# Linear attention and a gated layer on one core: a new order for the head, chunk 0 alone beside the weight conversion, chunk 1 by seven products

## The chip, the cores and the metric

The kernel runs on one core of a Trainium2 chip. The metric is the device time of one execution in microseconds (us), given as the median of several executions. Profiles come from one execution taken by the hardware profiler. TensorE is called PE in the profile, its weight loads PEld, VectorE DVE, ScalarE ACT, GpSimd POOL, and SyncE, which issues the DMAs, SP.

## The reference

```python
# q, k, v: (8 batches, 8 heads, 576 rows, 64), g_norm: (64,)
kv  = einsum('bhsd,bhse->bhde', k, v)
o   = einsum('bhsd,bhde->bhse', q, kv)
o   = o / sqrt(mean(o * o, axis=-1) + 1e-6) * g_norm
x   = o.transpose(0, 2, 1, 3).reshape(4608, 512)
out = (sigmoid(x @ w_gate) * (x @ w_val)) @ w_out      # w_gate, w_val: (512, 1536), w_out: (1536, 512)
```

q, k and v are float32. The three weight matrices arrive as float64 and are converted to float32 in the kernel by operations on their bits; every matmul is float32.

## The kernel before

**Attention.** Work comes in pairs of heads: n = 4 x batch + pair, n from 0 to 31. `attention(n, at_ps)` returns eleven steps: `kv_mm` (L227, k transposed times v on PE) and `kv_out` (L233, two copies on DVE, which also issues the k and v loads of a later n), `q_mm` (L241, six transposes on PE) and `q_out` (L246, copy on ACT, issues q of a later n), `u_mm` (L256, q times kv on PE), `u_square` (L260, ACT), `u_sum` (L264, DVE), `u_root` (L268, square root on ACT), `u_norm` (L271 and L273, DVE), `x_mm` (L282, transposes on PE) and `x_out` (L291, ACT, writes the columns of `xT`). The matrix x is kept transposed in `xT[c]`, where chunk c is 512 of the 4608 rows. A batch has 576 rows, so chunk 0 lies wholly in batch 0 (n = 0 to 3), and chunk 1 has the last 64 rows of batch 0 and 448 rows of batch 1 (n = 4 to 7). `xT[c][:, m, :]` comes from pair m.

**Weights.** There are 18 units, in `units`: twelve named ("gv", f), each with 128 columns of w_gate and of w_val, and six named ("wo", f) with two blocks of 128 rows of w_out. `load_unit(u)` issues two DMAs (L106) of 512 KB into one of NST = 3 buffers `st`. `convert(u)` gives five steps: s0 (L139 on DVE, then L141 on ACT), s1 (L147 on DVE, L149 on ACT), s2 (L154, DVE), s3 (L158, DVE) and s4 (L163, DVE). Before, s4 of each unit but the first also issues the next load that has not been issued, and s0 and s1 of the unit u + 1 stand in the order ahead of s2 to s4 of unit u.

**Matmuls.** A block (c, f) of the first layer makes 128 columns of the hidden layer for a chunk. In the plain form (`Plain`, L400) it is eight matmuls with 512 columns moving, four (m = 0 to 3) for the gate and four for the value, followed by a sigmoid on ACT (`gate`, L405) and a product on DVE (`end`, L408), which are put into `late` and run amid the next block. The plain second layer (`second_layer`, L385) makes each 128-row tile t of the output by twelve matmuls. The fast form (`first_layer_fast` L526, `second_layer_fast` L606) splits rows, columns and depth in halves and makes seven products in place of eight, each on 256 columns; it needs sums of the weights (`w_sum`, L512, on POOL, for the first layer; `t2w` on DVE, for the second, once for all chunks), sums of x (`x_sums`, L502 to L505, DVE), and sums of the hidden layer (`h_sums`, DVE). Its PSUM tiles are read by DVE at L538 to L559 between two products that add into the same tile, and a block of it ends at L562.

**Order.** The schedule is by hand: each engine works through its own instructions in the order in which the program writes them. Before, `stage(i)` runs the attention steps of the first eight pairs (NE = 8) as a software pipeline, with five conversion steps in the first three stages; then comes block (0, 0), then twenty plain blocks that alternate between chunks 0 and 1, while `convert_some` spreads the conversion over them. Then follow the whole second layer of chunk 0, the last three first-layer blocks of chunk 1 in the plain form, and chunk 1's second layer in the fast form. Chunks 2 to 8 are in the fast form throughout. The attention of the next batch is queued in `fill` by `feed`, and `slot()` takes one entry of it after certain matmuls; for batch 2 the slots lie in chunk 0's second layer and chunk 1's last blocks. The memory of the raw weights (`raw`) is given back after the last conversion step and used by the sums (`sums`).

Of the kernel before, what the change touches and what calls it, by code (L numbers as in the profile page):

```python
# [19 lines left out]
def kernel(  # L20
# [11 lines left out]
    nc = tc.nc  # L32
# [74 lines left out]
            else:  # L107
                nc.sync.dma_start(out=st[:, i], in_=moe_w_out[P * (f + i):P * (f + i) + P, :])

    def load_next_unit():  # L110
        load_unit(len(staged))

    def words(u):
        t = staged[u].rearrange("p i f -> p (i f)").bitcast(U32).rearrange("p (n two) -> p n two", two=2)
        return t[:, :, 0], t[:, :, 1]
# [8 lines left out]
    def convert(u):  # L124
        kind, f = units[u]
        vec = nc.vector
        d = {}

        def s0():

            t = const.tile([P, 2, DM], FP32, name=f"{kind}{f}") if kind == "gv" else w2[:, f:f + 2, :]
            if kind == "gv":
                for i, name in enumerate(("wg", "wv")):
                    w[name, f] = t[:, i].rearrange("p (m f) -> p m f", m=NMT)
            else:
                for i in range(2):
                    w["wo", f + i] = t[:, i]
            d["m"] = m = t.rearrange("p i f -> p (i f)")
            vec.tensor_scalar(out=m.bitcast(U32), in0=words(u)[1], scalar1=0x000FFFFF, scalar2=None,  # L139
                              op0=ALU.bitwise_and)  # L140
            nc.scalar.activation(out=m, in_=m.bitcast(U32), func=AF.Identity, scale=2.0 ** -20, bias=one)  # L141

        def s1():


            d["p"] = p = raw.tile([P, UW], U32, tag="cz", name="cz", bufs=2)
            vec.tensor_scalar(out=p, in0=words(u)[1], scalar1=20, scalar2=0x7FF, op0=ALU.logical_shift_right,  # L147
                              op1=ALU.bitwise_and)
            nc.scalar.activation(out=p.bitcast(I32), in_=p, func=AF.Relu, scale=2.0 ** 23, bias=exp_off)  # L149

        def s2():

            m = d["m"]
            vec.scalar_tensor_tensor(out=m, in0=words(u)[0], scalar=2.0 ** -52, in1=m, op0=ALU.mult, op1=ALU.add)  # L154

        def s3():
            p = d["p"]
            vec.scalar_tensor_tensor(out=p, in0=words(u)[1], scalar=0x80000000, in1=p, op0=ALU.bitwise_and,  # L158
                                     op1=ALU.bitwise_or)

        def s4():
            m = d["m"]
            vec.tensor_tensor(out=m, in0=m, in1=d["p"].bitcast(FP32), op=ALU.mult)  # L163
            if u:
                load_next_unit()

        return [s0, s1], [s2, s3, s4]


    halves_of = [convert(u) for u in range(len(units))]  # L170
    converts, last = deque(), {}
    converts.extend(halves_of[0][0] + halves_of[0][1] + halves_of[1][0])
    last[0] = 5
    for u in range(1, len(units)):
        if u + 1 < len(units):
            converts.extend(halves_of[u + 1][0])
        converts.extend(halves_of[u][1])
        last[u] = len(converts)
    made = [0]

    def convert_some(n):
        for _ in range(min(n, len(converts))):
            converts.popleft()()
            made[0] += 1

    def converted(u):
        convert_some(last[u] - made[0])

    for n in range(4):
        load_kv(n)  # L190
        load_q(n)
        if n == 0:
            load_next_unit()


    w2 = const.tile([P, NFT, DM], FP32, name="w2")
# [6 lines left out]
        nc.scalar.dma_start(out=g_col[HD * e:HD * e + HD], in_=g_norm.rearrange("(d o) -> d o", o=1))  # L203
    make_identity(nc, ident)
    nc.vector.memset(eps, 1e-6)
    for kv in kvs:
        nc.vector.memset(kv, 0.0)

# [90 lines left out]
    def slot():  # L299
        if fill:  # L300
            fill.popleft()()
# [26 lines left out]
    def flush():  # L328
        while fill:
            fill.popleft()()  # L330
# [7 lines left out]
    def sg_tile():  # L338
        return sb.tile([P, G], FP32, tag="sg", name="sg", bufs=4)
# [17 lines left out]
    def at_ps(kind):  # L357
        return psum_at.tile([P, 2, 512], FP32, tag="at", name="at")

    def two(i):  # L360
        return at_ps(None) if i == 3 else psum0.tile([P, 2, 512], FP32, tag=f"two{i}", name="two")

    shared = [None]
    turns = {"u": 1, "qx": 0}

    def early(kind):

        if kind == "q":
            return shared[0]
        tag = "u" if kind == "u" else "qx"  # L370
        t = two(turns[tag] if tag == "u" else 2 + turns[tag])
        turns[tag] = 1 - turns[tag]
        if kind == "kv":
            shared[0] = t
            return t[:, :, JH * P:]
        return t

    def mm_ps():
        return psum.tile([P, 512], FP32, tag="mm", name="mm", bufs=6)

    def second_layer(c):
        for t in range(G // P):
            ps = mm_ps()
            for f in range(NFT):
                nc.tensor.matmul(ps, gv[c, f][:, P * t:P * t + P], w["wo", f], start=(f == 0), stop=(f == NFT - 1))  # L385
                if f % 2:
                    slot()
            ot = sg_tile()
            nc.scalar.copy(out=ot, in_=ps)
            store(c, t, ot)  # L390


    class Plain:
# [15 lines left out]

    late = deque()  # L410

    def finish():
        while late:
            late.popleft()()

    def halves(t):
        return t[:, 0], t[:, 1]

    def plain(c, f, n_convert, ps):

        converted(f)
        blk = Plain(c, f, ps)
        for at in range(2 * NMT):
            i, m = divmod(at, NMT)
            blk.mm(i, m)
            slot()
            if late:
                late.popleft()()
            convert_some(n_convert * (at + 1) // 8 - n_convert * at // 8)
        late.extend([blk.gate, blk.end])  # L430


    KV, KV_OUT, Q, Q_OUT, U, U_SQUARE, U_SUM, U_ROOT, U_NORM, X, X_OUT = range(11)
    a = [attention(n, early) for n in range(NE)]

    def do(n, *steps):
        if 0 <= n < NE:
            for step in steps:
                a[n][step]()

    def stage(i, n_convert):
        do(i, KV, Q, KV_OUT, Q_OUT)
        do(i - 2, U_SUM, U_ROOT, U_NORM)
        do(i - 1, U, U_SQUARE)
        do(i - 3, X, X_OUT)
        convert_some(n_convert)

    for i in range(NE + 1):
        stage(i, 2 if i < 2 else 1 if i == 2 else 0)
        if i + 5 == NE:  # L450
            load_next_unit()
            load_next_unit()
    blk = Plain(0, 0, halves(early("u")))
    for m in range(NMT):
        blk.mm(0, m)
    do(NE - 1, U_SUM, U_ROOT)
    do(NE - 2, X, X_OUT)
    do(NE - 1, U_NORM)
    convert_some(2)
    for m in range(2):  # L460
        blk.mm(1, m)
    do(NE - 1, X, X_OUT)
    for m in range(2, NMT):
        blk.mm(1, m)
    convert_some(2)
    blk.gate()
    first_ctx.__exit__(None, None, None)
    hp = ctx.enter_context(tc.tile_pool(name="hp", bufs=21))
    blk.end()
    blocks = [(1, 0)] + [(c, f) for f in range(1, NFT - 3) for c in range(2)] + [(0, f) for f in range(NFT - 3, NFT)]  # L470
    for n, (c, f) in enumerate(blocks):
        plain(c, f, 5, halves(two(n % 4)))
    assert n % 4 == 3
    finish()
    convert_some(len(converts))
    psum_ctx.__exit__(None, None, None)
    psum = ctx.enter_context(tc.tile_pool(name="psum", bufs=1, space=bass.MemoryType.PSUM))
    raw_ctx.__exit__(None, None, None)


# [149 lines left out]
    def sums_of(c):  # L630
        if c < NG:
            fill.append(lambda: fill.extendleft(reversed(x_sums(c))))


    sums = ctx.enter_context(tc.tile_pool(name="sums", bufs=2, side="right"))
    b12, b11, b21, b22 = (w2[:, NF2 * (j - 1):NF2 * j, DH * (n - 1):DH * n] for j, n in ((1, 2), (1, 1), (2, 1), (2, 2)))
    t2w = {i: sums.tile([P, NF2, DH], FP32, name=f"t2w{i}", bufs=1) for i in (2, 3, 4)}
    t2w[1] = b12
    tt(out=t2w[3], in0=b22, in1=b12, op=ALU.subtract)
    feed(2, at_ps)  # L640
    second_layer(0)
    for n in (1, 2, 3, 4):
        for f in (0, NF2):
            w_sum(f, n)
    for f in range(NFT - 3, NFT):
        plain(1, f, 0, (mm_ps(), mm_ps()))
        if f == NFT - 3:
            tt(out=t2w[1], in0=b12, in1=b11, op=ALU.subtract)
            tt(out=t2w[2], in0=b22, in1=t2w[1], op=ALU.subtract)
            tt(out=t2w[4], in0=b21, in1=t2w[2], op=ALU.subtract)  # L650
            for i in range(NF2 - 3):
                h_sums(1, i)
    finish()
    for i in range(NF2 - 3, NF2):
        h_sums(1, i)
    flush()
    sums_of(2)
    second_layer_fast(1)
    flush()


    for c in range(2, NG):
        if c + 1 < B:
            feed(c + 1, at_ps)
        first_layer_fast(c)
        sums_of(c + 1)
        second_layer_fast(c)
        flush()
# [30 lines left out]
```

## Time and profile before

| What | Value |
|---|---|
| Median of 9 runs | 1128.75 us (1128.31 to 1130.16) |
| Profiled execution | 1128.31 us |
| its span, first to last instruction | 1126.2 us |
| granted PE clock | 1.00 |
| PE busy | 1105.9 us, 98% |
| DVE / ACT / POOL busy | 536.8 / 310.6 / 239.6 us |
| HBM read / written | 47.19 / 9.44 MB |

The span is what the engines' instructions cover; the execution's own time is 2.1 us longer. The page cuts the span into 40 slices of about 28 us and gives the busy share of each engine in tenths. A group line names the source line, the engine, the operation, the tiles written and read, the count, then total busy time, the mean of one in ns and the idle time before it. A line of the chain of waits has the start, the length and what the chain passed through. A line of the timeline has the start, the length, the engine and the instruction, and in brackets how long the engine stood idle before it and what released it. Lines of SPq are DMA issues.

### The profile page before, as it was taken

The numbers are of one execution on the slowest core, as the hardware profiler recorded it, in microseconds if no ns is written. First come the engines' busy times: TensorE is split into PE (matmuls) and PEld (weight loads), VectorE is DVE, ScalarE is ACT, GpSimd is POOL, SyncE is SP. The second block draws the span as 40 slices with busy tenths as digits, with TensorE's granted clock in tenths as the row PEclk, the third lists the DMA queues.
The fourth block names the chain that finished last, engine by engine and source line by source line (L and its number), as shares of the span: only waits on it lengthen the run. The fifth ranks groups of instructions, "written<-read, shape, count | busy, mean of one in ns | idle before, by whom it ended". The sixth has DMA issues, their size and how long they took to land.

```text
span 1126.2 us, 14586 instructions
## 1 busy us (share of the span) xinstructions
PE 1105.9 (98%) x5616; PEld 884.7 (79%) x5616; DVE 536.8 (48%) x1087; ACT 310.6 (28%) x589; POOL 239.6 (21%) x342
## 2 busy tenths in 40 slices
PE   6999999999999999999999999999999999999998
PEld 5644444547888888888888888888888888888887
DVE  4567664054155524562355425551655246615641
ACT  4633340223033303331243113330334021101110
POOL 0000001000033303330133104320333034404420
PEclk9999999999999999999999999999999999999999
DMA  9844331120202012110202120201200000010001
GB/s 244 211 140 134 137 112 36 47 71 14 77 22 54 11 29 63 46 30 19 72 12 54 27 75 12 53 12 42 55 11 6 19 19 1 1 27 12 1 1 38
DMA packets 71588, 57.56 MB, mean 51 GB/s; under 512 B 40800, under 2 KB 65376, under 8 KB 71520
## 3 DMA queue, kind: packets, MB, share of 16 engines
q1 hardware_dynamic: 71360, 56.64, 19.0%
q8 instruction: 45, 0.74, 0.3%
q14 instruction: 23, 0.19, 0.1%
q10 hardware_dynamic: 160, 0.00, 0.0%
HBM read 47.19 MB, written 9.44 MB: 50 GB/s over the span
## 4 chain that ended last, share of the span: by engine, by line
PE 95%; DVE 2%; DMA 1%; ACT 1%; SPq 0%; issue 0%; ACTq 0%; DVEq 0%
PE mm L526 45%; PE mm L606 26%; PE two L400 9%; PE mm L385 4%; PE at L400 3%; PE at L256 2%; PE at L227 2%; PE at L241 1%; PE at L282 1%; PE mm L400 1%; DMA q<-in_q_dram 1%; DMA v<-in_v_dram 1%; PE two L256 0%; DVE sq L273 0%; DVE gv L163 0%; DVE ms L264 0%
## 5 line engine op out<-in xcount | busy, mean ns | idle before, releaser
L512 POOL TENSOR_TENSOR tw<-gv 128x256 f32<-128x256 f32 x168 | 120.6, 729 | 835.7 <-PE mm L526 655.6
L526 PE MATMUL mm<-sx,tw 128*128 128x256 f32 x672 | 159.7, 380 | 0.0
L526 PE MATMUL mm<-xT,tw 128*128 128x256 f32 x672 | 159.5, 380 | 0.0
L526 PE MATMUL mm<-xT,gv 128*128 128x256 f32 x672 | 158.7, 379 | 0.0
L526 PEld LDWEIGHTS mm<-xT,gv 128*128 128x128 f32 x672 | 127.7, 190 | 17.4
L526 PEld LDWEIGHTS mm<-sx,tw 128*128 128x128 f32 x672 | 126.1, 190 | 16.7
L526 PEld LDWEIGHTS mm<-xT,tw 128*128 128x128 f32 x672 | 125.3, 190 | 16.1
L512 POOL TENSOR_TENSOR tw<-gv,tw 128x256 f32<-128x256 f32 x168 | 123.6, 757 | 0.0
L400 PE MATMUL two<-xT,gv 128*128 128x512 f32 x256 | 111.3, 593 | 2.1 <-DVE gv L163 1.6
L400 PEld LDWEIGHTS two<-xT,gv 128*128 128x128 f32 x256 | 48.3, 190 | 62.4 <-issue 61.9
L606 PE MATMUL mm<-t2w,gv 128*128 128x256 f32 x384 | 89.0, 379 | 0.0
L606 PE MATMUL mm<-w,gv 128*128 128x256 f32 x384 | 88.1, 379 | 0.0
L606 PE MATMUL mm<-w,s 128*128 128x256 f32 x384 | 88.1, 379 | 0.0
L555 ACT ACTIVATE sg<-sg 128x256 f32<-128x256 f32 x84 | 35.0, 417 | 191.7 <-DVE sg L554 191.7
L606 PEld LDWEIGHTS mm<-w,s 128*128 128x128 f32 x384 | 73.0, 190 | 9.9
L606 PEld LDWEIGHTS mm<-t2w,gv 128*128 128x128 f32 x384 | 72.6, 190 | 9.7
L606 PEld LDWEIGHTS mm<-w,gv 128*128 128x128 f32 x384 | 72.5, 190 | 9.6
L526 PE MATMUL mm<-sx,gv 128*128 128x256 f32 x336 | 79.4, 379 | 0.0
L546 DVE TENSOR_TENSOR gv<-mm,sg 128x256 f32<-128x256 f32 x84 | 35.7, 425 | 88.9 <-PE mm L526 88.9
L533 ACT COPY sg<-mm 128x256 f32<-128x256 f32 x84 | 31.3, 372 | 141.0 <-PE mm L526 140.9
L526 PEld LDWEIGHTS mm<-sx,gv 128*128 128x128 f32 x336 | 63.1, 190 | 8.2
L562 DVE TENSOR_TENSOR gv<-gv,sg 128x512 f32<-128x512 f32 x84 | 67.2, 840 | 0.2
(93 smaller groups left out, 1150.8 us busy)
## 6 DMA issues: line engine op xcount, KB each, us to landing
k<-in_k_dram SPq DMA_DIRECT2D x32, 288.0 KB, 4.5
v<-in_v_dram SPq DMA_DIRECT2D x32, 288.0 KB, 5.0
q<-in_q_dram SPq DMA_DIRECT2D x64, 144.0 KB, 3.2
st<-in_moe_w_gate_dram SPq DMA_DIRECT2D x12, 512.0 KB, 3.8
st<-in_moe_w_val_dram SPq DMA_DIRECT2D x12, 512.0 KB, 5.0
st<-in_moe_w_out_dram SPq DMA_DIRECT2D x12, 512.0 KB, 4.0
out_dram<-sg SPq DMA_DIRECT2D x24, 192.0 KB, 2.3
out_dram<-sg SPq DMA_DIRECT2D x24, 128.0 KB, 2.3
```

The lines of the kernel that those rows point to most:

```text
L227: nc.tensor.matmul(ps[HD * e:HD * e + HD, 0, 0:HD], pairs[n]["k"][:, e, js], pairs[n]["v"][:, e, js], start=(j == 0), stop=(j == NJ - 1))
L241: nc.tensor.transpose(ps[:, j // JH, c0:c0 + NP], pairs[n]["q"][:, j].rearrange("p e d -> p (e d)"), ident[0:NP, 0:NP])
L256: nc.tensor.matmul(d["u"][:, i], qT[:, M * i:M * i + MU], kvs[n % 2], start=True, stop=True)
L385: nc.tensor.matmul(ps, gv[c, f][:, P * t:P * t + P], w["wo", f], start=(f == 0), stop=(f == NFT - 1))
L400: nc.tensor.matmul(self.ps[i], w[("wg", "wv")[i], self.f][:, m, :], xT[self.c][:, m, :], start=(m == 0), stop=(m == NMT - 1), skip_group_c ...
L512: nc.gpsimd.tensor_tensor(out=tw[f, i], in0=b[in0], in1=b[in1] if isinstance(in1, tuple) else tw[f, in1], op=ALU.subtract)
L526: nc.tensor.matmul(ps, wt[:, m, :], xs[:, m, :], start=(new and m == 0), stop=(m == NK - 1), skip_group_check=True)
L533: nc.scalar.copy(out=d["sg"][:, h2], in_=pa)
L546: tt(out=d["h"][:, h2], in0=pb, in1=d["sg"][:, h2], op=ALU.add)
L555: nc.scalar.activation(out=d["sg"][:, h2], in_=d["sg"][:, h2], func=AF.Sigmoid)
L562: tt(out=d["h"], in0=d["h"], in1=d["sg"], op=ALU.mult)
L606: nc.tensor.matmul(ps, hs(f), ws[:, f, :], start=(new and f == 0), stop=(f == NF2 - 1), skip_group_check=True)
```

## The change

The order of the first eight pairs is now written out as a string of tokens. The number in a token is n: `K0` is `kv_mm` and `q_mm` of pair 0, `KVO0` and `QO0` are its two copies, then `U0`, `SQ0`, `SUM0`, `ROOT0`, `NORM0`, `X0` and `XO0` are the other steps by their names. `c` is the next conversion step, `w1` and `w2` issue the loads of units 1 and 2, and `bfim` (as `b012`) is one matmul of block (0, f): i = 0 for the gate and 1 for the value, m the quarter of the depth. `G` and `E` are the sigmoid and the product of block (0, 0). The PSUM tiles of the head are shared differently: one tile for k, v and q of all pairs, one each for even and odd pairs, and one for block 0.

Conversion now goes unit by unit, five steps each, and s4 of each unit u issues the load of unit u + 3, that of unit 0 included. Blocks 2 to 11 of chunk 0 follow, with one unit converted per block. Chunk 0's second layer then has f outermost: its four output tiles are summed side by side in four PSUM tiles, and the six "wo" units are converted beside it; its last two f are done tile by tile, with the sums of x for chunk 1 in the slots. All of chunk 1 is in the fast form. The `t2w` sums are cut into eight halves and queued ahead of batch 2's attention, which is now fed into chunk 1's first layer. A Sqrt on one unused column is issued on ACT at the start.

```diff
-    def load_next_unit():
-        load_unit(len(staged))
...
-            if u:
-                load_next_unit()
-        return [s0, s1], [s2, s3, s4]
-    halves_of = [convert(u) for u in range(len(units))]
-    converts, last = deque(), {}
...
+            load_unit(u + NST)
+        return [s0, s1, s2, s3, s4]
+    STEPS = 5
+    converts = deque(step for u in range(len(units)) for step in convert(u))
...
+    nc.scalar.activation(out=sb.tile([P, 1], FP32, name="unused", bufs=1), in_=eps, func=AF.Sqrt)
...
     def plain(c, f, ps):
         converted(f)
         blk = Plain(c, f, ps)
         for at in range(2 * NMT):
+            blk.mm(*divmod(at, NMT))
+            if at in (0, 2) and late:
+                late.popleft()()
+            if at < STEPS:
+                convert_some(1)
+        late.extend([blk.gate, blk.end])
...
-    for i in range(NE + 1):
-        stage(i, 2 if i < 2 else 1 if i == 2 else 0)
...
+    order = """
+        K0 QO0 KVO0 U0 c c SQ0 c SUM0 K1 c ROOT0 NORM0 X0 QO1 KVO1 w1 c U1 XO0 K2 SQ1 SUM1 b000 KVO2
+        ROOT1 QO2 NORM1 b010 U2 X1 SQ2 K3 XO1 SUM2 ROOT2 b001 KVO3 QO3 w2 NORM2 U3 X2 SQ3 K4 XO2 SUM3
+        ROOT3 b011 KVO4 QO4 NORM3 U4 c X3 SQ4 K5 XO3 SUM4 c ROOT4 b002 KVO5 QO5 NORM4 U5 c X4 SQ5 K6 XO4
+        SUM5 ROOT5 b012 KVO6 QO6 NORM5 U6 c X5 SQ6 K7 XO5 SUM6 ROOT6 b003 KVO7 QO7 NORM6 U7 c X6 SQ7
+        b013 XO6 SUM7 b100 c ROOT7 b110 G NORM7 b101 E X7 c b111 XO7 c b102 b112 c b103 c b113
+    """
...
-    blocks = [(1, 0)] + [(c, f) for f in range(1, NFT - 3) for c in range(2)] + [(0, f) for f in range(NFT - 3, NFT)]
-    for n, (c, f) in enumerate(blocks):
-        plain(c, f, 5, halves(two(n % 4)))
...
+    late.extend([blks[1].gate, blks[1].end])
+    at0 = at_ps(None)
+    plain(0, 2, [at0[:, i] for i in range(2)])
...
+    for f in range(3, NFT):
+        plain(0, f, (mm_ps(), mm_ps()))
+    ps = [mm_ps() for _ in range(G // P)]
+    def second(t, f):
+        nc.tensor.matmul(ps[t], gv[0, f][:, P * t:P * t + P], w["wo", f], start=(f == 0), stop=(f == NFT - 1),
+                         skip_group_check=True)
+    for f in range(0, NFT - 2, 2):
+        converted(NFT + f // 2)
+        for at in range(2 * G // P):
+            second(at % (G // P), f + at // (G // P))
             if late:
                 late.popleft()()
+            if at < STEPS:
+                convert_some(1)
...
+    for n in (1, 2, 3, 4):
+        for f in (0, NF2):
+            w_sum(f, n)
+    fill.extend(x_sums(1))
+    for t in range(G // P):
+        for f in range(NFT - 2, NFT):
+            second(t, f)
+            slot()
+        ot = sg_tile()
+        nc.scalar.copy(out=ot, in_=ps[t])
+        store(0, t, ot)
...
-    tt(out=t2w[3], in0=b22, in1=b12, op=ALU.subtract)
-    feed(2, at_ps)
-    second_layer(0)
...
-    for f in range(NFT - 3, NFT):
-        plain(1, f, 0, (mm_ps(), mm_ps()))
...
-    second_layer_fast(1)
+    def t2w_sum(i, in0, in1):
+        for fs in (slice(0, NF2 // 2), slice(NF2 // 2, NF2)):
+            fill.append(lambda fs=fs: tt(out=t2w[i][:, fs], in0=in0[:, fs], in1=in1[:, fs], op=ALU.subtract))
+    t2w_sum(3, b22, b12)
+    t2w_sum(1, b12, b11)
+    t2w_sum(2, b22, t2w[1])
+    t2w_sum(4, b21, t2w[2])
...
-    for c in range(2, NG):
+    for c in range(1, NG):
```

More of the change, by code (lines that the diff above doesn't have):

```diff
@@ L163, in s4 @@
             vec.tensor_tensor(out=m, in0=m, in1=d["p"].bitcast(FP32), op=ALU.mult)
-            if u:
-                load_next_unit()
-        return [s0, s1], [s2, s3, s4]
-    halves_of = [convert(u) for u in range(len(units))]
-    converts, last = deque(), {}
[L172 to L178, printed above, removed]
+            load_unit(u + NST)
+        return [s0, s1, s2, s3, s4]
+    STEPS = 5
+    converts = deque(step for u in range(len(units)) for step in convert(u))
     made = [0]
@@ L186, in converted @@
     def converted(u):
-        convert_some(last[u] - made[0])
+        convert_some(STEPS * (u + 1) - made[0])
     for n in range(4):
@@ L192 @@
         if n == 0:
-            load_next_unit()
+            load_unit(0)
     w2 = const.tile([P, NFT, DM], FP32, name="w2")
@@ L358, in at_ps, with early, ps @@
         return psum_at.tile([P, 2, 512], FP32, tag="at", name="at")
[L360 to L376, printed above, removed]
+    def early(n):
+        shared = []
+        def ps(kind):
+            if kind == "q":
+                return shared[0]
+            t = psum0.tile([P, 2, 512], FP32, tag="kq" if kind == "kv" else f"ux{n % 2}", name="two")
+            if kind == "kv":
+                shared.append(t)
+                return t[:, :, JH * P:]
+            return t
+        return ps
     def mm_ps():
         return psum.tile([P, 512], FP32, tag="mm", name="mm", bufs=6)
[L381 to L390, printed above, removed]
     class Plain:
@@ L410, with plain @@
     late = deque()
[L412 to L419, printed above, removed]
+    def plain(c, f, ps):
         converted(f)
@@ L423, in plain @@
         for at in range(2 * NMT):
-            i, m = divmod(at, NMT)
-            blk.mm(i, m)
-            slot()
+            blk.mm(*divmod(at, NMT))
[4 more added lines that the diff above has]
+        late.extend([blk.gate, blk.end])
+    KV, KV_OUT, Q, Q_OUT, U, U_SQUARE, U_SUM, U_ROOT, U_NORM, X, X_OUT = range(11)
+    a = [attention(n, early(n)) for n in range(NE)]
+    steps = {"K": (KV, Q), "KVO": (KV_OUT,), "QO": (Q_OUT,), "U": (U,), "SQ": (U_SQUARE,), "SUM": (U_SUM,),
+             "ROOT": (U_ROOT,), "NORM": (U_NORM,), "X": (X,), "XO": (X_OUT,)}
@@ new lines, with block01 @@
+    """
+    blks = {}
+    def block01(f):
+        if f not in blks:
+            t = psum0.tile([P, 2, 512], FP32, tag="kq", name="two") if f else at_ps(None)
+            blks[f] = Plain(0, f, [t[:, i] for i in range(2)])
+        return blks[f]
+    for token in order.split():
+        name = token.rstrip("0123456789")
+        n = token[len(name):]
+        if name == "b":
+            block01(int(n[0])).mm(int(n[1]), int(n[2]))
+        elif name == "c":
+            convert_some(1)
+        elif name == "w":
+            load_unit(int(n))
+        elif name == "G":
+            blks[0].gate()
+        elif name == "E":
+            blks[0].end()
+        else:
+            for step in steps[name]:
+                a[int(n)][step]()
+            if token == "K7":
+                first_ctx.__exit__(None, None, None)
+                hp = ctx.enter_context(tc.tile_pool(name="hp", bufs=21))
@@ new lines @@
+    late.extend([blks[1].gate, blks[1].end])
+    at0 = at_ps(None)
+    plain(0, 2, [at0[:, i] for i in range(2)])
+    psum_ctx.__exit__(None, None, None)
+    psum = ctx.enter_context(tc.tile_pool(name="psum", bufs=1, space=bass.MemoryType.PSUM))
+    for f in range(3, NFT):
[4 more added lines that the diff above has]
+                         skip_group_check=True)
@@ L427, in plain @@
+    for f in range(0, NFT - 2, 2):
+        converted(NFT + f // 2)
+        for at in range(2 * G // P):
+            second(at % (G // P), f + at // (G // P))
             if late:
                 late.popleft()()
[L429 to L446, printed above, removed]
-    for i in range(NE + 1):
-        stage(i, 2 if i < 2 else 1 if i == 2 else 0)
[L450 to L469, printed above, removed]
-    blocks = [(1, 0)] + [(c, f) for f in range(1, NFT - 3) for c in range(2)] + [(0, f) for f in range(NFT - 3, NFT)]
-    for n, (c, f) in enumerate(blocks):
-        plain(c, f, 5, halves(two(n % 4)))
@@ L473 @@
[L473 to L477, printed above, removed]
+            if at < STEPS:
+                convert_some(1)
     raw_ctx.__exit__(None, None, None)
@@ L638 @@
     t2w[1] = b12
-    tt(out=t2w[3], in0=b22, in1=b12, op=ALU.subtract)
-    feed(2, at_ps)
-    second_layer(0)
-    for n in (1, 2, 3, 4):
-        for f in (0, NF2):
-            w_sum(f, n)
-    for f in range(NFT - 3, NFT):
-        plain(1, f, 0, (mm_ps(), mm_ps()))
[L647 to L657, printed above, removed]
-    second_layer_fast(1)
-    flush()
-    for c in range(2, NG):
+    def t2w_sum(i, in0, in1):
[6 more added lines that the diff above has]
+    for c in range(1, NG):
         if c + 1 < B:
```

## The prediction

> **What bounds the kernel now.** I read the page first (engine shares, 40 slices), then the chain of waits in order of time, which separates stretches where TensorE runs without a gap from those where it waits, then the timeline of the head.
>
> ```profile
> PE 1105.9 (98%) x5616; PEld 884.7 (79%) x5616; DVE 536.8 (48%) x1087; ACT 310.6 (28%) x589; POOL 239.6 (21%) x342
> DMA  9844331120202012110202120201200000010001
> ```
> TensorE is the bound; DMA is busy only in the first two slices (28 us each). So time can be won by fewer matmuls, or in the head. The chain prices both:
>
> ```profile
> 49.21 0.94 ACT xT L291 x3
> 50.14 1.03 ACT gv L141
> 51.18 1.03 ACT cz L149
> 52.23 1.28 ACT L405
> 53.52 0.61 ACT sg L405
> 54.15 0.69 DVE gv L408
> 54.84 1.13 DVE gv L154
> 55.98 1.15 DVE cz L158
> 57.15 1.24 DVE gv L163
> 58.52 3.67 PE two L400 x8
> ...
> 264.42 36.27 PE mm L606 x168
> 300.69 1.73 PE mm L526 x8
> ...
> 904.75 72.52 PE mm L526 x336
> ```
> Until 58.52 the end is set by attention, ACT and VectorE (here unit 1's conversion, L141 to L163), with two blocks done. From there TensorE is dense. Each fp32 matmul is two records (L385: 48 matmuls, x96); the dense pieces give 20.60/48 = 0.429 us per 512-column record and 72.52/336 = 0.216 per 256-column record. Chunk 2 begins at 300.69, and nothing after it is changed. So the question is when chunk 2 begins.
>
> **The dense part.** Chunk 1's first layer was 12 blocks x 16 records x 0.429 = 82.4 us; by seven products it is the 72.5 of the row at 904.75: -9.9. Its second layer already was the 36.3 at 264.42. Chunk 0 keeps its work: a block 6.87, a second layer 96 x 0.429 = 41.2. Batch 2's attention moves from chunk 0's second layer into chunk 1's first; dense pieces in the chain give 2 x 1.55 (L227) + 4 x 0.50 (L241) + 4 x 1.09 (L256) + 4 x 0.50 (L282) = 11.5 either way. Call X the time at which blocks 0 and 1 of chunk 0 are done and block 2 can start. Then chunk 2 begins at X + 10 x 6.87 + 41.2 + 11.5 + 72.5 + 36.3 = X + 230.2, plus new stalls. Before, 58.52 to 300.69 is 242.2: the 9.9, and 2.0 of stalls (1.2 of them at 253.02, TensorE waiting for a norm behind L648 to L650) that go.
>
> **The head: X.** Two loads move. SP issues in order: w1 puts unit 1 behind n = 5, and the last conversion step of unit 0 now issues unit 3's load directly behind it, ahead of n = 6 and 7. Before, units 1 and 2 stood behind n = 7:
>
> ```profile
> 30.43 0.83 SPq L106 DMA_DIRECT2D st<-in_moe_w_gate_dram  x1
> 36.02 0.69 PE L241 MATMUL at<-ident,q 96*128 96x96 f32 x6 [0.45 <-DMA q<-in_q_dram]
> ```
> A unit is 1.05 MB; the DMA view moved 313 to 349 GB/s while units flowed: 3.1 us each. n = 7 landed at 36.0; n = 6 I put one issue step earlier (k of n = 4 and 5 issued at 15.35 and 18.87): 32.5. Two units ahead make 38.7 and 42.2, and unit 2 lands at 45.3. At 250 GB/s, the rate of the k, v, q stretch, a unit is 4.2 and n = 7 comes at 44.4; if the units cost nothing, at 36.0. I take 42.2, since the pace with units was seen. SP's new wait (unit 0's last step, about 18.3 on VectorE) is over when SP, held back by the DMA, gets there (issue of q for n = 5 ended at 22.3, unit 1 takes 2.4 more: 24.7); each us past that delays n = 6, n = 7 and unit 2.
>
> Up to K6 TensorE has, from k of n = 1 at 12.05: 5 attentions at 3.56 (L227 0.92, L241 0.71, L256 1.27, L282 0.66, warm rows) = 17.8, five block matmuls at 0.86 = 4.3, 2.0 waiting for the first norm, and 1.5 of cold matmuls (K1 took 1.55 where K4 took 0.92): 37.7, so n = 6 at 38.7 decides. The blocks fill gaps that before were idle. VectorE's s0 of unit 1 sits behind NORM3 at about 32.0, and the unit lands at 29.0 + 3.1 = 32.1: no cost; later, SUM4, KVO5 and U5 queue behind it. The early Sqrt takes two table loads (1.28 us at 8.60 and 19.99) off ACT's path; DMA covers both, so I count 0.
>
> From K6: K6 and its transposes 1.63 to 40.3, b012 41.2, U6 42.5, X5 43.1, K7 44.7, b003 45.6, U7 46.9. Square 0.70 to 47.6; SUM7 0.82 behind s4 of unit 1 on VectorE, 48.5; s0 of unit 2 0.69 to 49.2, its ACT half 1.15 to 50.35, ahead of ROOT7 (0.30, 50.65); NORM7 1.05 to 51.75. G's table load and sigmoid 1.28 + 0.60 end at 52.55, E 0.69 at 53.25, then s1 0.69 and s2, s3, s4 at 1.22: 57.6. TensorE does X6, b013, b100, b110, b101, X7 (52.4) and five more block matmuls to 56.7. Unit 2 is last: with 0.14 to TensorE, X = 57.7. Low end 54 (n = 7 early, VectorE waits closed), high end 62 (units at 250 GB/s +2.2, cold blocks +2).
>
> **Beside the blocks.** A unit costs VectorE 0.69 + 0.69 + 1.22 + 1.22 + 1.22 = 5.04, the product that ends a block 0.69: 5.73 per block of 6.87 (before, about one unit per two blocks). Order in VectorE: s0, s1, end of block f-1, s2, s3, s4 of f+1. The end waits for block f-1; s4 follows 0.15 + 0.69 + 3.66 = 4.5 later, and block f+1 starts 6.87 later: 2.4 us of cover, if s0, s1 and their ACT halves ran earlier. Zero cost; without that cover see the second rival.
>
> Second layer with f outermost: 16 records per pair of f, 6.87, against 5.04 of conversion. It begins at 126.4, the last unit is ready by 126.4 + 0.8 + 5 x 5.04 = 152.4 and needed at 160.7. Eight weight sums on POOL (0.73 each, 5.8) wait for that, end at 158.2, and are needed after 167.6; uncovered they cost 5.8. The four sums on x (0.69 each) lie under the last 6.87.
>
> [...]
>
> **New stall in chunk 1.** The sums t2w come as eight halves of 1.76/2 = 0.88 in the first eight slots. VectorE works 42.2 us in the 72.5 of the row at 904.75, 7.0 per pair of blocks; seven halves make 13.2 against 12.09. It lags 1.1 into the next pair, whose second product adds into a tile that VectorE must first have read: I take 1.0. Low end 0; high end 7.0, if all eight halves come on top. POOL works beside them:
>
> ```profile
> L562 DVE TENSOR_TENSOR gv<-gv,sg 128x512 f32<-128x512 f32 x84 | 67.2, 840 | 0.2
> ```
> This 840 ns is 0.69 where POOL is idle (L502, same shape): 0.15 each, or 1.2 for eight. [...]
>
> **Sum.** 57.7 + 230.2 + 1.0 = 288.9 against 300.7: -11.8. The profiled execution took 1128.31 (span 1126.2 + 2.1); the median is 1128.75, 0.44 above. 1128.75 - 11.8 = 1117.0.
>
> **Rivals.** (1) Head early: if units delay n = 7 little, X is near 54.5: -15, 1113.7. For: units moved faster than k, v, q. Against: the DMA row is full. 0.15.
> (2) Conversion sets the pace, the slower case: if s0, s1 and ACT's halves do not run ahead, the step is 4.65 + 1.38 + 2.3 = 8.3 per block, 1.46 over 6.87, ten times 14.6: +2.8, 1131.6. It decides from 8.05 per block. For: VectorE idles behind L405 now (50 us in 18 waits). Against: s0 and s1 need only a landed unit. 0.08.
> (3) Head late: X 61 to 62, -8, 1120.8. For: two units ahead of n = 6, and long in-order queues on VectorE. Against: n = 7's own row. 0.16.
> [...]
> (5) Half of (2), or a late seam at chunk 1, eats the gain: 0.04, no change.
>
> **How the numbers follow.** Forecast 0.55, rivals as given. Range 1112 to 1122: the forecast with X from 55 to 60 and 0 to 3 of stall, most of (1) and (3). No change is within 0.2%, 2.3 us, about what a measurement here can tell. Faster: forecast, (1), (3), 0.86; same 0.04; slower (2), (4), 0.10.
>
> **What would show it.** Right: chunk 2 begins near 289; 336 records at 0.216 in chunk 1's first layer; blocks 2 to 11 follow every 6.87 without a TensorE wait for L163; q of n = 7 ends a wait near 42; VectorE's last conversion stands before 155. Wrong: waits of TensorE for L163 at each block (2), X past 60 (3), a second layer longer than 41.5 (4), or a wait of more than 3 us in chunk 1's first two block pairs.

## The result and the profile after

The changed kernel took 1123.55 us in the median of 10 runs against 1129.19 of before (31 runs): ratio 0.9949, 95% interval 0.9941 to 0.9957, so some 5.8 us faster where 11.8 was forecast. The profiled execution took 1122.44 us, its span 1120.7. Line numbers have moved: K is L217 and L231 now, U L246, X L272, KVO L223, QO L236, the blocks L375, the second layer L451, the seven products L510, conversion L136 to L160.

The page after, the engines' busy time:

```profile
PE 1099.1 (98%) x5760; PEld 912.2 (81%) x5760; DVE 570.8 (51%) x1155; ACT 317.9 (28%) x613; POOL 279.7 (25%) x390
```

TensorE is busy 6.8 us less and still 98%. The chain of waits after (start, length, what) says where the three forecast times lie:

```profile
61.51 7.11 PE at L375 x16
68.61 61.80 PE mm L375 x144
130.41 41.20 PE mm L451 x96
171.61 8.65 PE mm L510 x40
...
295.17 1.73 PE mm L510 x8
```

Block 2 starts at 61.5, chunk 1 at 171.6, chunk 2 at 295.2 (before: 300.7). From 61.51 to 171.61 TensorE has no gap: 110.1 us, forecast 68.7 + 41.2 = 109.9. What is missing lies at both ends: X, the time at which block 2 can start, is 61.5 in place of 57.7, and chunk 1 takes 123.6 us where 72.5 + 36.3 + 11.5 + 1.0 = 121.3 was forecast. 3.8, 2.3 and the 0.2 between them make the 6.3 us by which chunk 2 begins later than the 288.9 forecast.

The head, from the timeline (start, length, engine, what; in brackets the idle time before it and its releaser):

```profile
11.48 0.69 DVE L136 TENSOR_SCALAR gv<-st 128x1024 uint32<-128x1024 uint32 x1 [1.67 <-DMA st<-in_moe_w_val_dram]
...
13.50 1.55 PE L217 MATMUL two<-v,k 96*64 96x64 f32 x24 [1.08 <-DMA v<-in_v_dram]
...
18.17 1.19 PE L272 MATMUL two<-ident,sq 115*128 115x115 f32 x5 [1.92 <-DVE sq L263]
...
19.16 2.34 PE L246 MATMUL two<-kv,qT 128*116 128x128 f32 x10
...
33.80 1.35 PE L246 MATMUL two<-kv,qT 128*116 128x128 f32 x10 [0.41 <-ACT qT L236]
34.02 0.68 DVE L136 TENSOR_SCALAR gv<-st 128x1024 uint32<-128x1024 uint32 x1
...
37.96 1.15 ACT L146 ACTIVATE cz<-cz,exp_off 128x1024 int32<-128x1024 uint32 x1 [0.55 <-DVE cz L144]
...
39.21 0.62 ACT L236 COPY qT<-two 128x576 f32<-128x576 f32 x1
...
39.88 1.35 PE L246 MATMUL two<-kv,qT 128*116 128x128 f32 x10 [1.85 <-ACT qT L236]
...
41.65 0.92 PE L217 MATMUL two<-v,k 96*64 96x64 f32 x24
...
46.29 0.92 PE L217 MATMUL two<-v,k 96*64 96x64 f32 x24
...
55.75 0.69 PE L272 MATMUL two<-ident,sq 115*128 115x115 f32 x5 [1.31 <-DVE sq L263]
```

The first row is s0 of unit 0 on VectorE, 13.50 is K1, 18.17 X0, 34.02 s0 of unit 1. K6 (41.65) and K7 (46.29) wait for no DMA. U4 (33.80) waits 0.41 us for its QO, U5 (39.88) 1.85: QO5 stands on ACT behind L146, the ACT half of a conversion step, and a root (L258) behind that. X7 (55.75) waits 1.31. U1 at 19.16 takes 2.34 us where a later pair takes 1.35.

TensorE has three waits in chunk 1. Below them stand four rows of VectorE's timeline:

```profile
191.32 1.97 PE L510 MATMUL mm<-xT,tw 128*128 128x256 f32 x8 [0.70 <-DVE gv L522]
...
231.94 1.97 PE L510 MATMUL mm<-xT,tw 128*128 128x256 f32 x8 [0.35 <-DVE gv L522]
...
245.61 0.71 PE L231 MATMUL at<-ident,q 96*128 96x96 f32 x6 [0.81 <-DVE kv L223]
```
```profile
175.88 0.95 DVE L638 TENSOR_TENSOR t2w<-w 128x768 f32<-128x768 f32 x1
...
182.52 1.50 DVE L638 TENSOR_TENSOR t2w<-w 128x768 f32<-128x768 f32 x1
...
230.64 0.82 DVE L263 TENSOR_TENSOR sq<-at,ms 116x640 f32<-116x640 f32 x1
...
245.09 0.46 DVE L223 COPY kv<-at 64x64 f32<-64x64 f32 x2
```

A t2w half takes 0.95 us while POOL rests and 1.50 while POOL makes weight sums (from 179.46). The last half ends at 190.8, just ahead of the first wait. Behind each wait the first matmuls take about 0.2 us more (1.97 for eight in place of 1.73).

### The profile page after: what moved, and what is told of

The parts are those of the page before. It is cut to its first block, busy times and chain, and to the rows that moved or that the text cites. A ratio compares the mean times of both kernels' runs of the same rounds, so it can differ in the third digit from the quotient of the medians.

```text
span 1120.7 us, 15097 instructions
## 1 busy us (share of the span) xinstructions
PE 1099.1 (98%) x5760; PEld 912.2 (81%) x5760; DVE 570.8 (51%) x1155; ACT 317.9 (28%) x613; POOL 279.7 (25%) x390
## 4 chain that ended last, share of the span: by engine, by line
PE 95%; DVE 2%; ACT 1%; issue 1%; DMA 1%; SPq 0%; ACTq 0%; DVEq 0%
PE mm L510 51%; PE mm L590 26%; PE mm L375 6%; PE mm L451 4%; PE at L246 2%; PE at L217 2%; PE at L231 1%; PE at L272 1%; PE at L375 1%; PE two L246 1%; DMA st<-in_moe_w_val_dram 1%; PE two L375 0%; PE two L217 0%; PE two L272 0%; DVE gv L546 0%
## 5 line engine op out<-in xcount | busy, mean ns | idle before, releaser
L496 POOL TENSOR_TENSOR tw<-gv 128x256 f32<-128x256 f32 x192 | 140.3, 741 | 790.1 <-PE mm L510 627.8
L510 PE MATMUL mm<-xT,tw 128*128 128x256 f32 x768 | 182.4, 380 | 1.0 <-DVE gv L522 1.0
L510 PE MATMUL mm<-sx,tw 128*128 128x256 f32 x768 | 182.4, 380 | 0.0
L510 PE MATMUL mm<-xT,gv 128*128 128x256 f32 x768 | 181.6, 379 | 0.0
L510 PEld LDWEIGHTS mm<-xT,gv 128*128 128x128 f32 x768 | 145.5, 190 | 20.1 <-issue 0.5
L510 PEld LDWEIGHTS mm<-xT,tw 128*128 128x128 f32 x768 | 143.3, 190 | 20.3 <-issue 1.8
L510 PEld LDWEIGHTS mm<-sx,tw 128*128 128x128 f32 x768 | 144.1, 190 | 19.0
L496 POOL TENSOR_TENSOR tw<-gv,tw 128x256 f32<-128x256 f32 x192 | 144.6, 774 | 0.0
L510 PE MATMUL mm<-sx,gv 128*128 128x256 f32 x384 | 90.9, 379 | 0.0
L590 PEld LDWEIGHTS mm<-t2w,gv 128*128 128x128 f32 x384 | 72.5, 190 | 9.6
L510 PEld LDWEIGHTS mm<-sx,gv 128*128 128x128 f32 x384 | 72.1, 190 | 9.4
L543 DVE TENSOR_TENSOR gv<-mm,gv 128x256 f32<-128x256 f32 x96 | 40.7, 424 | 47.9 <-PE mm L510 47.5
L526 ACT ACTIVATE sg<-mm 128x256 f32<-128x256 f32 x96 | 36.3, 384 | 100.8 <-PE mm L510 100.8
```

Source lines behind the costliest of these rows:

```text
L496: nc.gpsimd.tensor_tensor(out=tw[f, i], in0=b[in0], in1=b[in1] if isinstance(in1, tuple) else tw[f, in1], op=ALU.subtract)
L510: nc.tensor.matmul(ps, wt[:, m, :], xs[:, m, :], start=(new and m == 0), stop=(m == NK - 1), skip_group_check=True)
L526: nc.scalar.activation(out=d["sg"][:, h1], in_=pa, func=AF.Sigmoid)
L543: tt(out=d["h"][:, h1], in0=pc, in1=d["h"][:, h1], op=ALU.add)
L590: nc.tensor.matmul(ps, hs(f), ws[:, f, :], start=(new and f == 0), stop=(f == NF2 - 1), skip_group_check=True)
```

## Experiments

Theories on the head: **queues** (what stands ahead in the engines' in-order queues sets X) against **loads** (units 1 and 3 ahead of n = 6 and 7 set it, as the prediction had it). On chunk 1: **VectorE's queue** against **the attention's steps**. Times of variants are compared by their medians and ratios to before; their profiles give the places.

**e1: the t2w halves early.** The eight halves are issued ahead of the last two f of chunk 0's second layer.

```diff
+    (t2w_sum runs its two halves at once, ahead of fill.extend(x_sums(1)))
-            fill.append(lambda fs=fs: tt(out=t2w[i][:, fs], ...))
+            tt(out=t2w[i][:, fs], ...)
```

> The eight t2w halves run on VectorE right after the last conversion, beside chunk 0's last matmuls of the second layer, where VectorE waited 11.5 us in the profile after. Theory 'VectorE queue' (the halves, up to 1.51 us each beside POOL, push the products of chunk 1's first blocks late, and TensorE waits at 191.3, 231.9 and 245.6): chunk 1's start to chunk 2's start falls from 123.6 to 120.3 to 121.2 us, the time by 2.4 to 3.3 us against the changed kernel. Rival 'batch 2's attention in a denser first layer' (the waits come from the attention's steps, not from the halves): only the first wait goes, 1.0 us, and the waits at 231.9 and 245.6 stay.

1120.03 us, ratio 0.9914 (0.9901 to 0.9927). VectorE's timeline and the chain of e1:

```profile
159.42 2.87 DVE L628 TENSOR_TENSOR w<-w 128x768 f32<-128x768 f32 x2
```
```profile
171.36 1.73 PE mm L510 x8
...
292.18 1.73 PE mm L510 x8
```

Chunk 1 takes 120.8 us, and all three waits of TensorE in it are gone: it was VectorE's queue, and the attention costs nothing when it begins at the first slot. But this edit does two things: it takes the halves out of the slots, and it lets batch 2's attention begin eight slots earlier, that is one pair of blocks and one slot, so that its steps meet other places of a pair. The first wait came right behind the halves. The other two came 41 and 55 us after the last half, right behind steps of the attention on VectorE (the norm L263 at 230.64, the copies L223 at 245.09). Which of the two things took those away, no run separates. The last six halves still take 1.44 us each, near the 1.50 beside POOL in the changed kernel, now where nobody waits.

**e2: unit 3's load behind unit 2's.**

```diff
-            load_unit(u + NST)
+            if u:
+                load_unit(u + NST)
-        ... KVO3 QO3 w2 NORM2 ...
+        ... KVO3 QO3 w2 w3 NORM2 ...
```

> Unit 3's load is issued behind that of unit 2, not ahead of the inputs of n = 6 and 7. Theory 'loads set the head' (the prediction's step): n = 6 and 7 land 3 us earlier and block 2 of chunk 0 starts 2 to 3 us before 61.5. Theory 'the engines' queues set the head' (no matmul of K6 or K7 shows a wait for a DMA): K6 and K7 stay where they are (41.7 and 46.3), block 2 within 0.5 us of 61.5, no change in time.

1123.87 us, ratio 0.9954 (0.9942 to 0.9966); the chain of e2:

```profile
62.15 7.10 PE at L376 x16
```

Block 2 comes no earlier, and U5 waits 2.58 us: unit 1 landed later here, and VectorE stood 0.63 us at its s0 (34.63). For n = 6 and 7 the loads theory falls in this order of the engines.

**e3: two conversion steps behind.**

```diff
-        SUM4 c ROOT4 b002 KVO5 QO5 NORM4
+        SUM4 ROOT4 b002 KVO5 QO5 c NORM4
-        b100 c ROOT7 b110 G NORM7 b101 E X7 c
+        b100 ROOT7 b110 G NORM7 c b101 E X7 c
```

> Two conversion steps are moved in the order: s1 of unit 1 behind QO5, so that its ACT half no longer stands ahead of ROOT4 and QO5, and s0 of unit 2 behind NORM7, so that its ACT half no longer stands ahead of ROOT7 and G. Theory 'the engines' queues set the head': the 1.85 us wait of U5 and the 1.31 us wait of X7 shrink, and block 2 starts 1.7 to 3 us before 61.5; the lower end if the inputs of n = 6, which landed about 41, then hold K6. Theory 'loads set the head': no more than 0.7 us, the time by which K6's inputs were early.

1120.82 us, ratio 0.9925 (0.9912 to 0.9937). Timeline, then chain, of e3:

```profile
38.09 1.35 PE L246 MATMUL two<-kv,qT 128*116 128x128 f32 x10 [0.47 <-ACT qT L236]
...
52.80 0.66 PE L272 MATMUL two<-ident,sq 115*128 115x115 f32 x5
```
```profile
58.41 7.10 PE at L375 x16
```

U5's wait falls from 1.85 to 0.47, X7 comes without its wait of 1.31, and block 2 comes 3.1 us earlier. The two waits make 2.7 of that; the rest goes with X0, which came 0.45 us earlier in this profile (17.72). The queues theory holds.

**e4: chunk 1's first layer plain.** `first_layer_fast(1)` is replaced by twelve plain blocks with the same slots.

> Chunk 1's first layer in the plain form, all else as changed (without the sums of x for chunk 1). The prediction's dense term: 192 records of 0.429 in place of 336 of 0.216, +9.9 us, less the 2.4 to 3.3 us of waits that the fast form with the t2w halves and the attention has: +6.6 to +9.9 us against the changed kernel. If the seven products bring less than their records say, under +5.

1131.33 us, ratio 1.0015 (1.0006 to 1.0025): by the ratios the seven products bring some 7.5 us in the change. Chunk 1 takes 130.7 us in this profile, so against e1's 120.8 they bring 9.9, the term of the prediction; the change lost the difference in its own waits. Without them, the new head and order would have bought nothing.

**e5: e1 and e3 together.**

> The t2w halves early (as in e1_t2w_early) and the two conversion steps behind (as in e3_steps_behind) together. If the two losses are separate, as their places say (head, chunk 1), they add: -3.5 and -2.7 against the changed kernel's 1123.6, 1117.3 us, block 2 at 58.4 and chunk 2 about 120.8 us after chunk 1. If one hides the other, 1119 to 1120.

1117.38 us, ratio 0.9891 (0.9876 to 0.9907). The two losses are separate and add. Block 2 starts at 58.39 and chunk 2 at 289.31, where the prediction had 57.7 and 288.9.

**e6: e5 with unit 3's load behind.**

> As e5_both, and unit 3's load behind unit 2's. With the conversion steps out of the way K6 waited 0.28 us at 40.06 for its inputs, and SP's loads are close behind the engines. Theory 'a second bound close behind the first': K6 and K7 come up to 1 us earlier than in e5_both, block 2 0.3 to 1 us earlier. Theory 'engines only': no difference to e5_both.

1118.38 us, ratio 0.9896 (0.9882 to 0.991): no gain that can be told. Its profile doesn't compare well: unit 0's s0 started at 12.89 there and at 10.57 in e5's, and block 2 came 2.4 us later (60.77).

**e7: without the early Sqrt.**

> The changed kernel without the early Sqrt on ACT. The prediction counted it at 0, because the inputs were to cover it. Theory 'the inputs cover it': block 2 within 0.5 us of 61.5, no change. Theory 'ACT is in the early chain' (L138, L146, the square and the root follow one another from 12.2 to 16.2): two table loads of 1.28 us come back, block 2 starts 1.3 to 2.6 us later. And if the early table load is what makes k and v of n = 1 land later than before (13.5 against 12.05), they land at 12.05 here.

1124.12 us, ratio 0.9938 (0.9924 to 0.9952), against 0.9949 with it: not told apart. n = 1 landed at 14.47 in this profile, so the early table load is not what makes it late. Block 2 started at 63.3, 1.8 us later, but not through the table loads: unit 0's s0 started 0.96 later (12.44), and X0 followed it after the same 6.69 us as in the changed kernel. The chain of e7 goes from the sum (L253, 15.97) through s3 of unit 0 on VectorE (16.79 to 17.92), behind which NORM0 stands, and not through the first root on ACT. The other 0.8 lies in K2, whose matmuls ran cold here (1.55 us in place of 0.96, its transposes 0.2 more).

**e8: block (0, 0) behind the batches.** The eight `b0im` stand together ahead of b100.

> The order of the changed kernel with the eight matmuls of block (0, 0) taken from amid the batches to behind them, ahead of b100. Theory 'the blocks fill waits of TensorE': a pair took 4.64 us with a block matmul of 0.86 inside, of which 0.41 was a wait for QO; without it the wait grows and the pair takes as long, so block 2 starts 5 to 7 us later. Theory 'a pair's matmuls set its pace': a pair takes 0.86 less, and block 2 starts within 1.5 us of 61.5.

1129.93 us, ratio 1.0008 (0.9994 to 1.0023): 6.4 us over the changed kernel. Its timeline shows the first theory's pace: from U2 to U3 it is 4.64 us without a block matmul, as from K6 to K7 in the changed kernel with one.

```profile
26.29 1.35 PE L246 MATMUL two<-kv,qT 128*116 128x128 f32 x10 [1.30 <-ACT qT L236]
...
30.93 2.42 PE L246 MATMUL two<-kv,qT 128*116 128x128 f32 x10 [1.30 <-ACT qT L236]
```

In its profile (its slowest run, 1135.96) block 2 came at 75.25, more than the waits explain. Three stretches of that profile (length, PE, PEld, DVE, ACT, POOL, granted clock, DMA, GB/s):

```profile
30.00:40.00 10.00, 7.77 (x86) 7.01 (x87) 4.19 (x10) 5.10 (x10) 0.00 (x0) 0.83 1.13 276
40.00:50.00 10.00, 5.96 (x54) 5.07 (x53) 6.52 (x13) 5.23 (x12) 0.00 (x0) 0.73 1.11 256
50.00:60.00 10.00, 8.70 (x60) 8.00 (x59) 4.19 (x7) 3.00 (x7) 0.00 (x0) 0.50 0.87 195
```

With 1.30 us of wait in each pair (2.75 in one) the granted clock fell from 1.00 to 0.50, and U took 2.48 us; in the changed kernel it was 1.00 all through the head. The twelve runs of e8 had a granted clock of 0.991 to 0.998, those of the changed kernel 0.997 to 1.00. So the blocks amid the batches fill waits, but how much of the 6.4 us is the waits and how much the clock, no run separates.

**e9: sixteen idle matmuls before X0, on e5.**

```diff
-        K0 QO0 KVO0 U0 c c SQ0 c SUM0 K1 c
+        d7 K0 d3 QO0 KVO0 U0 d2 c c SQ0 c SUM0 K1 d4 c     # d: matmuls of the identity by itself
```

> e5_both with sixteen matmuls of the identity by itself in TensorE's waits before X0 (7 before K0, 3 behind it, 2 behind U0, 4 behind K1); their output is read by nothing. Theory 'cold matmuls cost 1 us of the head': U1 takes 1.25 to 1.35 us in place of 2.34, X0 0.66 in place of 1.19, and all later pairs and block 2 come 1.0 to 1.6 us earlier than in e5_both (58.4), if n = 1 lands at the same time. Theory 'inputs close behind': K6's inputs hold the gain to 0.3 us.

1115.31 us, ratio 0.988 (0.9864 to 0.9896), the lowest median of all, though its interval overlaps e5's. Rows of e9's timeline:

```profile
17.99 1.26 PE L246 MATMUL two<-kv,qT 128*116 128x128 f32 x10
19.18 0.92 PE L217 MATMUL two<-v,k 96*64 96x64 f32 x24
...
56.21 7.11 PE L375 MATMUL at<-xT,gv 128*128 128x512 f32 x16 [0.65 <-ACT sg L380]
```

n = 1 landed as in e5 (12.67 and 12.66), and X0 came 0.2 later; U1 takes 1.26, K2 starts at 19.18 (e5: 20.51), and block 2 comes 2.2 us earlier than in e5. "Cold" here means matmuls that take longer than the same ones later. They cost more than the 1.0 to 1.6 expected, since K2 was cold too (1.55 in e5).

**e10: NORM0 ahead of s3 of unit 0, on e5; e11: with e9's matmuls; e12: and unit 3's load behind.**

```diff
-        K1 c ROOT0 NORM0 X0 QO1 KVO1 w1 c U1
+        K1 ROOT0 NORM0 X0 QO1 KVO1 w1 c c U1
```

> e5_both with s3 of unit 0 moved behind KVO1, so that NORM0 no longer waits 1.2 us for it on VectorE. Theory 'VectorE's order in the first pair': X0 comes 1.0 us after ROOT0's end plus 0.1, 1 to 1.2 us earlier against K1's start than in e5_both (17.25 to 12.66), U1 and block 2 too. Rival: unit 0, ready 1.2 us later, holds b000 and takes the gain back (in e5_both b000 ran 4.4 us behind the start of U1).

> Both of the two edits on e5_both. If they add and the inputs do not hold them, 1.5 to 2.5 us under e5_both's 1117.4; if the inputs of n = 6 and 7 (units 1 and 3 ahead of them) are the next bound, under 1 us, and K6 or K7 shows a wait for a DMA.

> e11_warm_norm0 with unit 3's load behind unit 2's. In e11_warm_norm0 K6 waited 0.49 us for a load at 40.09. Theory 'units 1 and 3 ahead of n = 6 and 7 are the second bound, just behind the engines': that wait goes, block 2 starts 0.5 to 1.5 us earlier than in e11_warm_norm0, the time falls to 1114 to 1116.5. Rival: the wait moves to the conversion of unit 1, whose load landed late in that run (U5 waited 1.76 us behind it), and nothing is gained.

e10: 1117.09 us, 0.9893 (0.9876 to 0.9909). X0 came 0.7 us earlier than in e5 with the same start of unit 0's s0 (10.57), chunk 1 0.9 us; in the time it can't be told. e11: 1117.35 us, 0.989 (0.9876 to 0.9905), nothing on top: U5 waited 1.76 us behind unit 1's conversion, K6 0.49 us for a load, and block 2 came at 59.15 (e10: 57.49). e12: 1118.01 us, 0.9892 (0.9876 to 0.9909), as its rival says; its timeline:

```profile
33.63 0.69 DVE L136 TENSOR_SCALAR gv<-st 128x1024 uint32<-128x1024 uint32 x1 [3.00 <-DMA st<-in_moe_w_val_dram]
...
38.12 1.39 PE L247 MATMUL two<-kv,qT 128*116 128x128 f32 x10 [3.56 <-ACT qT L237]
```

VectorE stands 3.0 us at s0 of unit 1, whose load has not landed, with the attention's steps behind it, and U5 waits 3.56. So loads are a second bound, a little behind the queues, through unit 1's place on VectorE above all. What e9's matmuls are worth depends on it: e9 shows 2.2 us in the head, e11 and e12 show nothing.

## Why the prediction was right and wrong

**The dense part was right.** 110.1 us measured, 109.9 written; 41.20 for the second layer with f outermost, where TensorE had no gap and a granted clock of 1.00, so rotating four PSUM tiles cost nothing. A lower clock in this layer, the prediction's (4), no run shows: in e1 and e5 the layer took 41.20 too. From block 2 to chunk 1 TensorE waits for no conversion: the cover was enough, and rival (2) fell. The seven products bring 9.9 (e4 against e1).

**The step that failed: "n = 6 at 38.7 decides".** TensorE was to reach K6 at 37.7, ahead of the load; it came at 41.65, behind it, and waited for no load there. The working had four terms too low:

- *The in-order queues before U5.* The prediction says that SUM4, KVO5 and U5 queue behind a conversion step and gives that no cost. U5 waited 1.85 us. It starts 5.86 or 5.87 us behind s0 of unit 1 in all six profiles with this order of that stretch (the changed kernel's, e1, e2, e4, e7, e8), whenever the earlier pairs ran: in e1 X0 came 1.0 us earlier and block 2 only 0.25. Moving this step and the one ahead of ROOT7, which the tail had counted, is worth 2.7 to 3.1 us of X (e3).
- *The first norm.* The working starts from k of n = 1 at 12.05 and adds 2.0 of wait for the norm. But X0 hangs on unit 0: it starts 6.68 or 6.69 us behind s0 of unit 0 in the ten profiles with this order of the first pair (the changed kernel's and e1 to e9), while s0 ranges from 10.46 to 12.89 and K1 from 12.62 to 15.15. The ACT halves of s0 and s1 stand ahead of SQ0, s3 ahead of NORM0; with s3 moved behind, it is 6.02 (e10). In the changed kernel s0 started at 11.48, in the one profile of before at 9.98. Why unit 0 lands at different times is open.
- *Cold matmuls* were put at 1.5 from K1 alone. The idle matmuls of e9, with which X0, U1 and K2 no longer run cold, are worth 2.2 of X on top of e5.
- *A pair* was 3.56 + 0.86 = 4.42 of TensorE's rows, one behind the other. It took 4.64, of which 0.41 is a wait for QO. The rows overlap, so the five attentions alone were written about 1 us too long, which hid part of the rest.

From K7 on the working held: 14.6 us from K7 to block 2 written, 15.2 measured, and unit 2's last step was the last to arrive (it ended at 61.36; the trace names the sigmoid of block 1, which ended at 61.38 but stands behind block 2's first matmul in the program). Rival (3) named the X that came, for a reason that e2 refutes (units ahead of n = 6) and one that e3 bears out (in-order queues).

**The stall in chunk 1:** 1.0 written, 123.56 - 120.3 = 3.3 measured. 0.5 of it is no stall, since chunk 1 takes 120.8 without any wait (e1) where the terms add to 120.3. The first wait, 0.70 with 0.24 behind it, is the one that the prediction priced at 1.0, though it came at the fourth product of the pair and not the second, and VectorE had more to do than counted; that the size fits is in part luck. What the prediction put at nothing are the other two waits, 1.8 us in all: steps of the attention that stand on VectorE where a new pair of blocks begins.

The 0.15 us for POOL's part was too low as well, a mean over 84 block ends most of which meet no POOL work: half of their 42 pairs meet none and take 1.28, eleven meet two POOL sums and take 2.08. In the changed kernel a t2w half that meets POOL's sums takes up to 1.51 us and a POOL sum there up to 1.44, against 0.95 and 0.73 alone; in e1 the last six halves took 1.44 each. That is nearer to the two one behind the other, 1.68 by these numbers, than to the row's 0.15 on top.

With both mended (e5), the time is 1117.4 us against 1117.0 written. That is in part luck: K7 starts 1.7 us later than written (44.80 and 43.1), and the tail behind it is 1.0 shorter, with a step that the prediction had counted ahead of ROOT7 now behind NORM7.

## What to carry to other kernels

In a hand-written order, go down each in-order queue and ask what stands ahead of the step that TensorE waits for: two moved tokens were worth about 3 us of the head, a moved load nothing. When a piece of work leaves a queue of slots, look at what moves up into its place. Put sums that are needed once where their engine idles, not into the first slots of the denser loop. And read a price for contention from the instructions that meet it, not from a mean over all of their kind.

## What the runs showed of the hardware that was not expected

- In e8 TensorE's granted clock fell amid work: with 1.30 us of wait in each pair (2.75 in one) it was 0.83, 0.73 and 0.50 in three successive stretches of 10 us, with U at 2.48 us in place of 1.35. In the changed kernel, with a block matmul in each pair and 0.41 of wait (1.85 in one), it stayed at 1.00.
- Matmuls whose result nobody reads shortened the head by 2.2 us (e9): U1 1.26 us in place of 2.34. With another order and other landings they brought nothing (e11). The granted clock reads 1.00 in these first stretches with and without them, so the slow matmuls show in the durations and not in that column.
- Where additions on VectorE and POOL met, both took longer: in the changed kernel t2w halves up to 1.51 us in place of 0.95, POOL's sums up to 1.44 in place of 0.73.
